# Up projection of a gated MLP by seven products with partial sums in PSUM, in a phase of its own, on one Trainium2 core

## The chip, the cores and the metric

The kernel runs on one core of one Trainium2 chip. The metric is device time in microseconds, as a median of runs. The core has five instruction streams that work side by side: TensorE (PE in the profile; PEld is its weight load), VectorE (DVE), ScalarE (ACT), GpSimd (POOL) and SyncE (SP), which here only starts transfers. TensorE writes into PSUM, eight banks of 128 x 512 fp32 numbers; VectorE and ScalarE read these; GpSimd works here on SBUF alone.

## What is computed

The inputs are x (2048 rows of 512), all in fp32. With xn = layernorm(x):

```python
qkv = xn @ wqkv                      # 512 -> 3*512, 32 heads of 16
# each position attends to 8 positions: itself and 2, 4, ..., 14 rows before it
logits = einsum(q, gathered k) * 16**-0.5 ;  attn = softmax(logits)
s = (attn applied to gathered v) @ wo            # 512 -> 512
h = relu(xn @ w1 + b1) ** 2                      # 512 -> 1792 : "up"
g = silu(h @ w2 + b2)                            # 1792 -> 512 : "down"
out = x + s * g
```

Every product is made with each operand as a sum of a high part (fp32r, a rounded copy) and a low part (operand minus high part): three matmuls, high*high, high*low and low*high (`PASSES`), in place of one.

## The kernel before

**Order of the work.** PE, V, A and G (lines 86 and 70 to 84) are wrappers that issue instructions for TensorE, VectorE, ScalarE and GpSimd and keep each engine's own order as written. A planner keeps two clocks, one for TensorE (227 ns for a matmul) and one for VectorE (elements / 0.96 + 170 ns). The attention is a generator (line 232) of VectorE work: for units of 256 rows a multiplication (`pr`, 128 x 2048), a reduction, softmax, a second multiplication (`pv`) and reduction. `pump(margin)` (line 359) takes pieces from it as long as VectorE's clock stays behind TensorE's plus the margin, so that attention fills VectorE between the things that TensorE waits for. `defer` (line 224) holds back ScalarE's part (an exponential, a start of a load) until TensorE's clock has come to a given time. Transfers on SyncE's queue are placed by the framework.

**Phase 1** (lines 539 to 647). x is normalized, turned (first four tiles on TensorE; later ones through a shuffle by DMA, `xb`, and a transpose on VectorE) and split into high (`A.activation`, line 469) and low (`lowx`, line 471). Sixteen tiles of 128 rows by three thirds of wqkv, 12 matmuls each, give q, k, v (`qkv`, line 477), which go out through ScalarE (`stg`) to DRAM and come back in the attention's layout (`load_u`, line 210). The turned tiles 4 to 15 are stored in DRAM as well (`sx`, line 602) and come back later as `xU` (`load_xT`, line 502). w1 and w2 are loaded in blocks of 128 rows of F and split by ScalarE and GpSimd (`next_w`, line 381).

**Phase 2** (lines 721 to 817) goes over four chunks of 512 rows. Per chunk, 14 steps f: `up(c, f)` (line 509) makes one block of h, 12 matmuls into a bank `ph`, after which ScalarE does relu with bias and two squares, and VectorE the low part (`lowh`, line 525); two steps later `down` (line 653) adds it into four banks `pb`, 12 matmuls. Between them lie the output products of the attention (`out_product`, line 689, 12 matmuls per tile, from `oq`, which is read back from `so` in DRAM, turned by VectorE and split) and the end: `gate` (silu) and `finish`, where VectorE multiplies, GpSimd adds x and a store follows. PSUM: four banks `acc`, two `h`, two `tp`.

Of the kernel before, what the change touches and what calls it, by code (L numbers as in the profile page):

```python
# [8 lines left out]
F32 = mybir.dt.float32  # L9
# [12 lines left out]
W = 8  # L22
# [14 lines left out]
Q0, Q1, K0, K1, V0, V1 = range(6)  # L37
HOME = {0: 10, 1: 6, 2: 7, 3: 8, 4: 9, 5: Q0, 6: Q1, 7: K0, 8: K1, 9: V0, 10: V1}
# [4 lines left out]
TURN = 4  # L43

# [8 lines left out]
def body(ctx: ExitStack, tc: tile.TileContext, x, wqkv, wo, w1, b1, w2, b2, out):  # L53
# [42 lines left out]
    xTa = ctx.enter_context(tc.tile_pool(name="xTa", bufs=1))  # L96
    keep = ctx.enter_context(tc.tile_pool(name="keep", bufs=1))
    wts = ctx.enter_context(tc.tile_pool(name="wts", bufs=1))
    hpool = ctx.enter_context(tc.tile_pool(name="ph", bufs=1))
# [5 lines left out]
    def psH(name):  # L105
        return psum.tile([P, 512], F32, name=name, tag="h", bufs=2)
# [23 lines left out]
    p1ctx = ExitStack()  # L130
    px, pstg, pxT = (p1ctx.enter_context(tc.tile_pool(name=n, bufs=1)) for n in ("px", "pstg", "pxT"))
    xins = {}


# [7 lines left out]

    def buffer(name, i):
        return wts.tile([P, 2, 2, 512], FR, name=name, tag=f"b{i}")


    wq = [buffer(f"wq{i}", i) for i in range(6)]
# [15 lines left out]
    def wq_parts(s, kt):  # L163
        w = wq[2 * s + kt // 2]
        return w[:, 0, kt % 2], w[:, 1, kt % 2], raws[s, kt]
# [36 lines left out]
    sx = {c: dram.tile([P, TPC, 2, KT, P], F32, name=f"sx{c}") for c in range(1, NCH)}  # L202
# [170 lines left out]
    w12 = {}  # L373

    def load_w(f):
        r1, r2 = (piece(f"{n}{f}") for n in ("w1r", "w2r"))
        dma(r1.rearrange("p (k c) -> p k c", c=P), w1[:, f * P:(f + 1) * P].rearrange("(k p) c -> p k c", p=P))
        dma(r2, w2[f * P:(f + 1) * P, :])
        raws[f] = r1, r2

    def next_w():

        f = len(w12)
        if f < NF:
            w12[f] = buffer(f"w{f}", HOME[f]) if f in HOME else p2.tile([P, 2, 2, 512], FR, name=f"w{f}")
            for i, r in enumerate(raws.pop(f)):
                split(w12[f][:, 0, i], w12[f][:, 1, i], r, G)
            if f + 2 < NF:
                load_w(f + 2)


    NT = S // P
    mv, means, rs, shifts, xn, xb, pTs, xt, xT, seen = ({} for _ in range(10))
# [50 lines left out]
    def place(t):  # L444
        if t < TPC:
            xt[t] = xT[0][:, t]
        else:
            xt[t] = pxT.tile([P, 2, KT, P], FR, name=f"xt{t}", tag="xt", bufs=4)
# [8 lines left out]
    def trans(t):  # L457
        place(t)
        pTs[t] = psT(f"pxT{t}")
# [9 lines left out]
        A.activation(xt[t][:, 0], pTs[t].rearrange("p (k n) -> p k n", k=KT), AF.Copy)  # L469

    def lowx(t):
        not_before(seen.pop(t))
        V.tensor_sub(xt[t][:, 1], pTs.pop(t).rearrange("p (k n) -> p k n", k=KT), xt[t][:, 0].bitcast(F32))
# [3 lines left out]
    def qkv(t, s, between=None, late=False):  # L477
# [5 lines left out]
        for n, (kt, a, b) in enumerate(order):  # L483
            PE.matmul(ps, xt[t][:, a, kt], wq[2 * s + kt // 2][:, b, kt % 2, :], start=n == 0, stop=n == 11)
            if between and n == 5:
                between()
        evacuate(t, s, ps)

    def evacuate(t, s, ps):
        if t % 2 == 0:  # L490
            stgs[s] = pstg.tile([P, 4, 2, P], F32, name=f"stg{t}_{s}", tag="stg", bufs=4)
# [10 lines left out]
    def load_xT(c):  # L502
        xT[c] = xTa.tile([P, TPC, 2, KT, P], FR, name=f"xU{c}", tag="xT")
        for j in range(0, TPC, 2):
            A.dma_start(xT[c][:, j:j + 2].bitcast(F32), sx[c][:, j:j + 2])

    hs = {}

    def up(c, f):
        ph = psH(f"ph{c}_{f}")  # L510
        n = 0
# [5 lines left out]
        if f == NF - 1 and c + 1 < NCH:  # L517
            load_xT(c + 1)
# [320 lines left out]
```

## Time and profile before

| what | value |
| --- | --- |
| median of three runs | 501.14 us (500.05 to 503.08) |
| profiled execution, span | 500.6 us |
| TensorE busy | 491.6 us, 98% |
| VectorE busy | 422.9 us, 84% |
| ScalarE busy | 212.2 us, 42% |
| GpSimd busy | 133.4 us, 27% |
| moved by DMA | 88.79 MB |

All but a few instructions are issued through the wrapper of line 82, so the profile's groups are told apart by the names of their tiles: `pq` is a bank of the qkv product, `ph` of up, `pb` of down, `pw` of the output product; `pr` and `pv` are the attention's products, `L` its weights; `w` are the split blocks of w1 and w2; `z` the gate and the result. A row of a group has engine, operation, output and inputs, shape, count, then busy time and the mean in ns of one, then the idle time in front of them and what ended it. In a timeline the first number is the start and the second the duration, in us. In the rows of stretches come the stretch, its length, the engine's busy time with its number of instructions, the granted clock, the share of DMA and GB/s.

### The profile page before, as it was taken

What the parts mean: (1) busy time and instruction counts of PE and PEld (TensorE: products, weight loads), DVE (VectorE), ACT (ScalarE), POOL (GpSimd) and SP (SyncE); (2) the same over time, 40 slices, a digit from 0 to 9 for tenths busy, and PEclk for the clock granted to TensorE, in tenths of its full rate; (3) what the DMA queues carried; (4) which work ended last, traced back from release to release, by engine and by line L of the source; (5) the groups of instructions that cost most, each with busy time, mean ns of one, the idle gap of its engine ahead of it and who ended that gap; (6) DMA issues with size and microseconds to landing.
All of it is one profiled execution on the core that took longest, in us unless ns stands there. A gap on an engine that the chain in (4) does not pass through costs nothing.

```text
span 500.6 us, 5874 instructions
## 1 busy us (share of the span) xinstructions
PE 491.6 (98%) x2154; PEld 402.8 (80%) x2154; DVE 422.9 (84%) x352; ACT 212.2 (42%) x377; POOL 133.4 (27%) x123
## 2 busy tenths in 40 slices
PE   8997999999999999999999999999999999999997
PEld 6876888888888888888888888888888888888886
DVE  5905599999889699997999998899999889996235
ACT  5526556652344465515424342441254256214331
POOL 1312255343427499200223002041300022220000
PEclk9998999999999999999999999999999999999999
DMA  8996989969966975644216416152333705121022
GB/s 292 283 287 187 324 293 332 289 200 331 310 234 236 206 252 140 201 168 158 101 26 241 156 44 259 67 216 68 117 126 97 269 2 199 43 84 64 22 84 85
DMA packets 48520, 88.79 MB, mean 177 GB/s; under 512 B 5372, under 2 KB 32364, under 8 KB 45676
## 3 DMA queue, kind: packets, MB, share of 16 engines
q1 hardware_dynamic: 44172, 54.87, 35.1%
q10 hardware_dynamic: 4320, 33.56, 18.8%
q8 instruction: 17, 0.28, 0.2%
q14 instruction: 11, 0.09, 0.0%
HBM read 57.94 MB, written 27.32 MB: 170 GB/s over the span
## 4 chain that ended last, share of the span: by engine, by line
PE 95%; DMA 3%; ACT 0%; DVE 0%; SPq 0%; issue 0%; POOL 0%; ACTq 0%; POOLq 0%
PE ph L82 30%; PE pb L82 30%; PE pq L82 25%; PE pw L82 9%; DMA xb<-xn 2%; DMA x<-in_A_x 1%; PE pxT L82 0%; SPq L455 0%; ACT scratch L82 0%; DVE z L82 0%; ACT xn L82 0%; DVE st L82 0%; POOL rs L82 0%; ACT stg L82 0%; DVE xn L82 0%
## 5 line engine op out<-in xcount | busy, mean ns | idle before, releaser
L82 PE MATMUL pb<-w,h 128*128 128x512 f32 x672 | 160.6, 389 | 0.0
L82 PEld LDWEIGHTS pb<-w,h 128*128 128x128 f32 x672 | 126.1, 188 | 26.2
L82 PE MATMUL ph<-xU,w 128*128 128x512 f32 x504 | 120.6, 389 | 0.0
L82 PEld LDWEIGHTS ph<-xU,w 128*128 128x128 f32 x504 | 94.6, 188 | 19.6
L82 ACT ACTIVATE ph<-ph,b1t 128x512 f32<-128x512 f32 x56 | 37.0, 660 | 159.6 <-PE ph L82 150.6
L82 PE MATMUL pq<-wq,xt 128*128 128x512 f32 x432 | 101.3, 395 | 0.0
L82 PEld LDWEIGHTS pq<-wq,xt 128*128 128x128 f32 x432 | 81.1, 188 | 19.7
L82 DVE TENSOR_TENSOR pr<-k,q 128x2048 f32<-128x2048 f32 x32 | 77.6, 2425 | 1.6 <-DMA q<-sq 1.2
L82 DVE TENSOR_TENSOR pv<-v,L 128x2048 f32<-128x2048 f32 x32 | 74.2, 2320 | 0.6
L82 DVE TENSOR_REDUCE L<-pr 128x128 f32<-128x2048 f32 x32 | 72.9, 2278 | 0.6
L82 DVE TENSOR_REDUCE v<-pv 128x256 f32<-128x2048 f32 x32 | 72.9, 2279 | 0.6
L82 DVE TENSOR_TENSOR h<-ph,h 128x512 fp32r<-128x512 f32 x56 | 38.0, 679 | 31.9 <-ACT ph L82 31.9
L82 PE MATMUL pw<-wot,oT 128*128 128x512 f32 (+1 forms) x204 | 45.9, 376 | 0.0
L82 POOL TENSOR_TENSOR z<-z,xr 128x512 f32<-128x512 f32 x12 | 25.5, 2127 | 67.1 <-DVE z L82 57.7
L82 PEld LDWEIGHTS pw<-wot,oT 128*128 128x128 f32 x204 | 36.8, 188 | 7.1
L82 ACT ACTIVATE stg<-pq 128x512 f32<-128x512 f32 x48 | 28.2, 593 | 31.4 <-PE pq L82 28.0
L82 POOL TENSOR_TENSOR w<-w1r,w 128x512 fp32r<-128x512 f32 x14 | 29.4, 2098 | 44.9 <-ACT w L82 40.0
L82 PE MATMUL ph<-xT,w 128*128 128x512 f32 x168 | 40.5, 390 | 0.0
L82 PEld LDWEIGHTS ph<-xT,w 128*128 128x128 f32 x168 | 31.5, 188 | 6.7
L82 PE MATMUL pq<-wq,xT 128*128 128x512 f32 x132 | 32.7, 408 | 3.6 <-ACT stg L82 3.6
L82 ACT ACTIVATE h<-ph 128x512 fp32r<-128x512 f32 x56 | 33.7, 602 | 1.8
L82 PEld LDWEIGHTS pq<-wq,xT 128*128 128x128 f32 x132 | 25.5, 196 | 10.3 <-ACT stg L82 4.1
(64 smaller groups left out, 330.4 us busy)
## 6 DMA issues: line engine op xcount, KB each, us to landing
k<-sk ACTq DMA_DIRECT2D x8, 1408.0 KB, 8.3
v<-sv ACTq DMA_DIRECT2D x8, 1408.0 KB, 6.5
sx<-xt SPq DMA_DIRECT2D x12, 512.0 KB, 6.2
xU<-sx ACTq DMA_DIRECT2D x6, 1024.0 KB, 8.6
x<-in_A_x SPq DMA_DIRECT2D x16, 256.0 KB, 4.5
sk<-stg SPq DMA_DIRECT2D x8, 512.0 KB, 4.5
sq<-stg SPq DMA_DIRECT2D x8, 512.0 KB, 5.8
q<-sq ACTq DMA_DIRECT2D x8, 512.0 KB, 9.0
```

Source lines behind the costliest of these rows:

```text
L82: return tc.keep_in_program_order(f(*a, **k))
```

## The change

**Up by seven products.** Up is taken out of the chunks and becomes a phase between qkv and down. w1 is taken in pairs of blocks (7 pairs of 2 x 128 columns, rows in two halves of 256) and x in pairs of tiles (rows in two halves of 128, columns in two halves of 256). Four blocks of the product of a 2 x 2 by a 2 x 2 block matrix come from seven block products in place of eight, with sums of blocks made beforehand: `sums` for x (one subtraction on VectorE, three operations on GpSimd) and `sums_parts` (high on ScalarE, low on GpSimd); `prep_a` and `prep_b` for w1. A group is (half of x's pairs, pair of blocks of w1): four pairs of tiles side by side, 512 columns, seven products of two halves of 128 rows by three passes, 42 matmuls. There are 14 groups.

**Partial sums stay in PSUM.** Three banks serve a group. Products are added to a bank which ScalarE or VectorE has already read: ScalarE copies a partial sum out with the bias (`c1`, `c2`), VectorE adds another bank to the copy, TensorE adds the next product to the bank. Two of the seven products of a group are issued within the group behind it.

**Relu passes through DRAM.** A block of up is stored after relu in `sr` (56 stores of 256 KB) and read back in the down phase (`load_h`); there `prep_h` squares twice on ScalarE and subtracts on GpSimd (it was VectorE).

**Space.** x's parts lie in `XA` (four pairs) and `XB` (the other four, through DRAM in `sx`, over the place of wqkv's parts); w1's parts in a ring of three, of which two are later h's buffers; w2's parts take `XA`'s place at the end of up. PSUM has six banks `acc` and two `tp`. Split blocks of w2 are made from the last groups of up to step 7 of the first chunk, by GpSimd and, for five of them, VectorE. Down has 14 steps per chunk with no up between them.

```diff
-Q0, Q1, K0, K1, V0, V1 = range(6)
+SLOT = {p: p if p < 2 else 2 + p % 2 for p in range(NP)}
+HERE, AWAY = (0, 1, 6, 7), (2, 3, 4, 5)
+A11, A12, A22, S1, S2, S3, S4 = range(7)
+B11, B21, B22, T1, T4, T3, T2 = range(7)
+GROUPS = [(0, 0), (0, 1), (0, 2), (1, 0), (1, 1), (1, 2), (0, 3), (0, 4), (1, 3), (0, 5), (1, 4), (0, 6), (1, 5), (1, 6)]
+PREP = {0: 2, 5: 3, 6: 4, 7: 5, 10: 6}
+RELU = 3000
...
-        return psum.tile([P, 512], F32, name=name, tag="acc", bufs=4)
+        return psum.tile([P, 512], F32, name=name, tag="acc", bufs=6)
...
+    def prep_a(fp):
+        W = ring(fp)
+        l, r = halves(fp)
+        A.activation(W[:, B11:B22, 0], l, AF.Copy)
+        A.activation(W[:, B22, 0], r[:, 1], AF.Copy)
+        G.tensor_sub(W[:, B11:B22, 1], l, W[:, B11:B22, 0].bitcast(F32))
+        G.tensor_sub(W[:, B22, 1], r[:, 1], W[:, B22, 0].bitcast(F32))
+        G.tensor_sub(l[:, 0], r[:, 0], l[:, 0])
+        G.tensor_sub(r[:, 0], r[:, 1], r[:, 0])
+        G.tensor_sub(r[:, 1], r[:, 1], l[:, 0])
+        G.tensor_sub(l[:, 1], l[:, 1], r[:, 1])
+
+    def prep_b(fp):
+        W = ring(fp)
+        for n, src in zip((T1, T3), halves(fp)):
+            A.activation(W[:, n:n + 2, 0], src, AF.Copy)
+            G.tensor_sub(W[:, n:n + 2, 1], src, W[:, n:n + 2, 0].bitcast(F32))
...
+    def sums(p):
+        a, b = (pTs.pop(t) for t in (2 * p, 2 * p + 1))
+        if p < TURN // 2:
...
+            A.activation(b, turn, AF.Copy)
+        t = xs[p]
+        V.tensor_sub(t[:, 2:], turned(a, slice(0, D), "p (b k n) -> p b k n"), t[:, :2])
+        G.tensor_add(t[:, 0], t[:, 0], t[:, 1])
+        G.tensor_add(t[:, 3], t[:, 2], t[:, 3])
+        G.tensor_sub(t[:, 1], t[:, 1], t[:, 2])
+
+    def sums_parts(p):
+        x, t = XA[:, SLOT[p]], xs.pop(p)
+        A.activation(x[:, S1:, 0], t, AF.Copy)
+        G.tensor_sub(x[:, S1:, 1], t, x[:, S1:, 0].bitcast(F32))
+        if p in AWAY:
+            dma(sx[p], x.rearrange("p c h k n -> p (c h k n)").bitcast(F32))
...
-    def lowh(f):
-        h, ph, t = hs[f]
-        not_before(t)
-        V.tensor_sub(h[:, 1], ph, h[:, 0].bitcast(F32))
...
+    def product(ps, W, w, X, x, start, stop):
+        n = 0
+        for k in range(2):
+            for a, b in PASSES:
+                PE.matmul(ps.rearrange("p (j n) -> p j n", n=P), W[:, w, a, k], X[:, :, x, b, k], start=start and n == 0,
+                          stop=stop and n == 5, skip_group_check=True)
+                n += 1
...
+    def relu(f, i, ab, z):
+        def go():
+            A.activation(z, z, AF.Relu)
+            out_r(f, i, ab, z)
+        defer(clock["V"] + RELU, go)
...
+    for gi in range(len(GROUPS) + 1):
...
+            product(ps, R, B11, X, A11, True, False)
+            A.activation(c1[:, 0], ps, AF.Identity, bias=bias(f1))
+            pump(LATE)
+        if before:
+            i0, fp0, R0, X0, ps0, c10, c20, q0 = before
+            not_before(held[0])
+            V.tensor_add(c20[:, 1], c20[:, 1], q0)
+            relu(2 * fp0 + 1, i0, 1, c20[:, 1])
+            product(ps0, R0, T4, X0, A22, False, True)
+            A.activation(c10[:, 1], ps0, AF.Relu, bias=bias(2 * fp0))
+            out_r(2 * fp0, i0, 1, c10[:, 1])
+            pump(LATE)
+        if gi in PREP:
+            prep_a(PREP[gi])
+        if group:
+            product(py, R, B21, X, A12, True, True)
+            pump(LATE)
+            V.tensor_add(c1[:, 0], c1[:, 0], py)
+            relu(f1, i, 0, c1[:, 0])
+            product(ps, R, T2, X, S2, False, False)
+            A.activation(c2[:, 0], ps, AF.Identity, bias=bias(f2))
+            pump(LATE)
+            product(q, R, T1, X, S1, True, False)
+            pump(LATE)
+        if before:
+            product(q0, R0, B22, X0, S4, False, True)
+            pump(LATE)
+            V.tensor_add(c20[:, 0], c20[:, 0], q0)
+            relu(2 * fp0 + 1, i0, 0, c20[:, 0])
+        if gi in PREP:
+            prep_b(PREP[gi])
...
+        if gi >= 13:
+            next_w2(G)
+            next_w2(V if gi == 13 else G)
+        if group:
+            product(ps, R, T3, X, S3, False, False)
+            A.activation(c2[:, 1], ps, AF.Identity, bias=bias(f2))
+            held[:] = [clock["PE"] + 900]
+            pump(LATE)
+            before = (i, fp, R, X, ps, c1, c2, q)
+        if gi == 13:
+            next_w2(G)
+            next_w2(G)
...
+    def prep_h(n, eng=None):
+        if n < NS:
+            hs[n] = h = hbuf[n % 4]
+            r = rbuf.pop(n)
+            A.activation(h[:, 0], r, AF.Square)
+            A.activation(r, r, AF.Square)
+            (eng or G).tensor_sub(h[:, 1], r, h[:, 0].bitcast(F32))
...
+        def step(f):
+            n = c * NF + f
+            prep_h(n + 2)
+            load_h(n + 3)
             if c == 0:
-                next_w()
-            up(c, f)
+                next_w2(V if f % 2 else G)
...
+                if 3 <= f < 7:
+                    split(wot[:, 0, f - 3], wot[:, 1, f - 3], rwo[(f - 3) // 2][:, (f - 3) % 2], G)
```

In phase 1 `sums(p)` is called behind the second `lowx` of a pair and `sums_parts(p)` behind the next product; `prep_a` and `prep_b` of the first two pairs of blocks lie in its last four rounds. The output products of three tiles of the chunk before move to steps 1, 6 and 8, and the last chunk keeps its three last steps for the end, tile by tile, as before.

More of the change, by code (lines that the diff above doesn't have):

```diff
@@ L458, in trans @@
         place(t)
-        pTs[t] = psT(f"pxT{t}")
+        if t < TURN or t % 2 == 0:
+            pTs[t] = psT(f"pxT{t}")
+        else:
+            xs[t // 2] = stgp.tile([P, 4, 2, P], F32, name=f"xs{t}", tag="stg", bufs=5)
+            pTs[t] = xs[t // 2][:, :2].rearrange("p b k n -> p (b k n)")
         if t < TURN:
@@ L575, in body @@
     constants()
+    sums(0)
     qkv(0, 0, lambda: highs(2, 0))
@@ L584, in body @@
     lowx(3)
+    sums(1)
+    sums_parts(0)
     stats(4)
@@ L588, in body @@
     qkv(0, 2)
+    sums_parts(1)
     norm(4)
@@ L613, in body @@
             trans(a + 2)
+        else:
+            load_away(0)
         pump(LATE)
@@ new lines, in view @@
+    def view(base, off, shape, **k):
+        n = 1
+        for d in k.values():
+            n *= d
+        return base[:, off:off + n].rearrange(shape, **k)
+    W0f, W1f = (rings[i].rearrange("p c h k n -> p (c h k n)") for i in (0, 1))
+    hbuf = [view(b, o, "p (h n) -> p h n", h=2, n=512) for b, o in ((W1f, 0), (W1f, 1024), (W1f, 2048), (W0f, 0))]
+    pxc2.close()
+    x21c.close()
+    p2 = ctx.enter_context(tc.tile_pool(name="p2", bufs=1, side="right"))
+    wot = p2.tile([P, 2, 4, 512], FR, name="wot")
@@ L715, in finish @@
         dma(tile_rows(out, t)[:, cols], z[:, cols])
-    wot = p2.tile([P, 2, 4, 512], FR, name="wot")
-    b2t = p2.tile([P, D], F32, name="b2t")
     dma(b2t, b2[None, :].to_broadcast([P, D]))
+    rwo = [p2.tile([P, 2, D], F32, name=f"rwo{i}", tag="rwo", bufs=2) for i in range(2)]
+    for i in range(2):
+        for q in range(4):
+            rows = wo[q * P + 64 * i:q * P + 64 * i + 64, :].rearrange("(g p) n -> p g n", g=2)
+            dma(rwo[i][32 * q:32 * q + 32], rows)
+    for n in range(3):
+        load_h(n)
+    prep_h(0)
+    prep_h(1)
     for c in range(NCH):
@@ L725, in body @@
         room = ROOM if c else ROOM0
-        for f in range(2, NF):
+        def step(f):
+            n = c * NF + f
+            prep_h(n + 2)
+            load_h(n + 3)
             if c == 0:
-                next_w()
-            up(c, f)
-            pump()
-            if c == 0 and f == 3:
-                rwo = [p2.tile([P, 2, D], F32, name=f"rwo{i}", tag="oT", bufs=2) for i in range(2)]
-                for i in range(2):
-                    for q in range(4):
-                        rows = wo[q * P + 64 * i:q * P + 64 * i + 64, :].rearrange("(g p) n -> p g n", g=2)
-                        dma(rwo[i][32 * q:32 * q + 32], rows)
+                next_w2(V if f % 2 else G)
+        for half in ((0, 1), (2, 3)):
+            for f in range(2):
+                if half[0] == 0:
+                    step(f)
+                for j in half:
+                    down(pb, c, f, j)
+                pump(room)
+            if half[0] == 0 and c:
+                out_product(t0 - 3, psT(f"pw{t0 - 3}"))
+                pump(room)
+        if c:
+            load_o(c * 2 - 1, True)
+        for f in range(2, NF - 3 if last else NF):
+            step(f)
             if c == 0:
-                if 6 <= f < 10:
-                    split(wot[:, 0, f - 6], wot[:, 1, f - 6], rwo[(f - 6) // 2][:, (f - 6) % 2], G)
+                if 3 <= f < 7:
+                    split(wot[:, 0, f - 3], wot[:, 1, f - 3], rwo[(f - 3) // 2][:, (f - 3) % 2], G)
             elif f == 2:
```

302 lines of the change are left out of this document (176 added, 126 removed).

## The prediction

> **What bounds the kernel now.** I read the page's busy shares and its chain of waits first, then that chain in order of time, then the groups by form, then stretches and timelines of VectorE (DVE) and GpSimd (POOL), the two engines that the change loads differently.
>
> ```profile
> span 500.6 us, 5874 instructions
> PE 491.6 (98%) x2154; PEld 402.8 (80%) x2154; DVE 422.9 (84%) x352; ACT 212.2 (42%) x377; POOL 133.4 (27%) x123
> PE 95%; DMA 3%; ACT 0%; DVE 0%; SPq 0%; issue 0%; POOL 0%; ACTq 0%; POOLq 0%
> ```
> ```profile
> 154.01 2.76 PE ph L82 x12
> 156.77 2.72 PE pb L82 x12
> ```
>
> TensorE is the path for 95% of the span, and twelve 512-column matmuls take 2.72 us: 227 ns each, back to back. So a matmul taken out is worth 227 ns, as long as nothing else becomes late. Two more views say what may become late.
>
> ```profile
> 45.40:457.60 412.20, 384.51 (x281) 1.00 0.54 179
> ```
>
> That is DVE from its first attention product to its last: 384.5 us of work in 412.2, so 27.7 us idle. DVE is nearly a second bound. What it may lose is read at the end:
>
> ```profile
> 457.62 0.53 SPq L312 DMA_DIRECT2D so<-v  x1
> 457.82 0.69 DVE L82 TENSOR_TENSOR h<-ph,h 128x512 fp32r<-128x512 f32 x1 [0.23 <-ACT ph L82]
> ...
> 460.65 2.52 SPq L674 DMA_DIRECT2D oq<-so  x4
> ...
> 463.15 1.08 ACT L82 ACTIVATE oT<-pT 128x512 fp32r<-128x512 f32 x2
> 463.87 1.28 DVE L82 TENSOR_TENSOR oT<-pT,oT 128x512 fp32r<-128x512 f32 x2
> ...
> 479.58 0.69 DVE L82 TENSOR_TENSOR h<-ph,h 128x512 fp32r<-128x512 f32 x1 [4.75 <-ACT ph L82]
> ...
> 491.16 5.75 PE L82 MATMUL pw<-wot,oT 128*128 128x512 f32 x36
> ```
> ```profile
> oq<-so SPq DMA_DIRECT2D x32, 128.0 KB, 3.4
> ```
>
> The last attention unit is stored at 457.6. Its four reads begin at 460.7, take 2.5 us to issue and 3.4 to land (466.0, taking one issue as 0.6), a transpose, a copy and a subtraction of some 0.65 us each follow (468.0), and from the start of the last output products to the end there are 500.6 - 491.2 = 9.4 us. DVE by itself would let the kernel end at 477.5: **23 us of room before, and after a gain of 19 only 4.**
>
> **The products.**
>
> ```profile
> L82 PE MATMUL ph<-xU,w 128*128 128x512 f32 x504 | 120.6, 389 | 0.0
> L82 PE MATMUL ph<-xT,w 128*128 128x512 f32 x168 | 40.5, 390 | 0.0
> L82 DVE TENSOR_TENSOR h<-ph,h 128x512 fp32r<-128x512 f32 x56 | 38.0, 679 | 31.9 <-ACT ph L82 31.9
> L82 DVE TENSOR_TENSOR z<-pb,b2t 128x512 f32<-128x512 f32 x16 | 10.5, 683 | 2.7 <-PE pb L82 2.6
> L82 ACT ACTIVATE ph<-ph,b1t 128x512 f32<-128x512 f32 x56 | 37.0, 660 | 159.6 <-PE ph L82 150.6 <-DVE pv L82 4.5 <-DVE mx_None L82 4.5
> L82 DVE TENSOR_TENSOR z<-z,xlast 128x256 f32<-128x256 f32 x2 | 0.9, 426 | 0.1
> L82 ACT ACTIVATE h<-ph 128x512 fp32r<-128x512 f32 x56 | 33.7, 602 | 1.8
> L82 POOL TENSOR_TENSOR w<-w1r,w 128x512 fp32r<-128x512 f32 x14 | 29.4, 2098 | 44.9 <-ACT w L82 40.0 <-DMA x<-in_A_x 4.9
> L82 POOL TENSOR_TENSOR w<-w2r,w 128x512 fp32r<-128x512 f32 x14 | 22.6, 1615 | 0.0
> ```
>
> Up has 504 + 168 = 672 matmuls. After the change it has 14 groups of seven products of six: 588. The operands keep their form (128x128 weights, four runs of 128 columns), so 84 matmuls at 227 ns go: **-19.0 us**, and TensorE alone would end at 481.6. All else is priced against that.
>
> **Inside the up phase** a group lasts 42 x 0.227 = 9.5 us. ScalarE has four copies out of PSUM (0.66 each, the row with b1t) and three relus (0.60, as h<-ph) in it, 4.4 us, and in five groups four copies of parts more: it fits. DVE has three additions (0.68, the row of z<-pb). But sums are added to a bank that has just been copied out: the sixth product of a group waits for a DVE addition, and the product on the group before waits for ScalarE's last copy, one product (1.36 us) after it was produced, so 0.66 us of copy and a hand-off have 1.36 us. A small operation in front (0.6) is hidden there, just. Parts of w1 come from POOL, 5.5 operations of 512 columns for each pair of blocks; in three places (pairs three, four and six) the first use is one group, 9.5 us, behind the start. At 1.3 us each that is 7.1 us, at 1.9 (below) 10.5: about 1 us late each time. I take **+3** (bounds: 0, all hidden; 14 x 2.3, one attention operation in front of an addition in every group, 32).
>
> **POOL and DVE.** POOL loses the 28 splits (52.0 us) and gets, in operations of 512 columns: sums and parts of x 28 (3.5 for each of eight pairs), parts of w1 38.5, splits of w2 nine, and the 56 subtractions for h, which were DVE's: 131.5. What that costs is in this stretch, where POOL had no pause, and in a free DVE row:
>
> ```profile
> 178.77 3.34 POOL L82 TENSOR_TENSOR w<-w1r,w 128x512 fp32r<-128x512 f32 x1
> 182.07 1.30 POOL L82 TENSOR_TENSOR w<-w2r,w 128x512 fp32r<-128x512 f32 x1
> 183.34 1.29 POOL L82 TENSOR_TENSOR wot<-rwo,wot 128x512 fp32r<-128x512 f32 x1
> 184.59 3.34 POOL L82 TENSOR_TENSOR w<-w1r,w 128x512 fp32r<-128x512 f32 x1
> ```
> ```profile
> 183.19 0.68 DVE L82 TENSOR_TENSOR h<-ph,h 128x512 fp32r<-128x512 f32 x1
> 183.79 2.98 DVE L82 TENSOR_TENSOR pr<-k,q 128x2048 f32<-128x2048 f32 x1
> 186.81 2.29 DVE L82 TENSOR_REDUCE L<-pr 128x128 f32<-128x2048 f32 x1
> 189.61 2.97 DVE L82 TENSOR_TENSOR pr<-k,q 128x2048 f32<-128x2048 f32 x1
> ...
> 242.20 2.29 DVE L82 TENSOR_TENSOR pr<-k,q 128x2048 f32<-128x2048 f32 x1
> ```
>
> An attention multiplication takes 2.98 instead of 2.29 us when a POOL operation is running at its start, and the POOL operation behind it waits until it has ended (3.34 instead of 1.29). The reduction keeps its 2.29. With a full queue POOL does three operations in 184.59 - 178.77 = 5.82 us: 1.94 us each.
>
> The Trainium skill ("SBUF — State Buffer", "Who interferes with whom") says why: a DVE instruction with two SBUF inputs and a GpSimd instruction that reads SBUF exclude one another for a whole instruction, whichever starts first. By that rule the additions from PSUM cost nothing extra; the rows agree (0.68 us for h<-ph while POOL is busy), and the rule speaks against handing DVE's work to POOL. Taken strictly it gives the time of rival 2 below; by the rows of before it gives two fifths of that loss.
>
> **The down phase on POOL.** A step of 12 matmuls is 2.72 us. In steps 0 to 7 of the first chunk POOL has eight subtractions for h, four splits of w2 and four of wo: 16 x 1.94 = 31.0 us in 21.8. Two steps of lead (5.4) cover part: **+4** (bounds: 0, at 1.29 each it is 20.6; and 9). At the change of phase the first h can be ready only behind what POOL still has of w2 (three or so at 1.3 to 1.9, against some 2 us of lead): **+2** (0 to 5). Later chunks have 14 + 4 + 2 operations in 49 us, 39 at 1.94: hidden, with no other cover than that. h's way through DRAM (14.7 MB out and back) puts reads on SyncE's queue behind stores that wait for DVE and POOL; those have about four steps (10.9 us) of lead against 3.4 to land and 3 for copies and POOL, so they are hidden until DVE is 4 us late; past that they pass its lateness on.
>
> **The start.**
>
> ```profile
> 23.81 0.78 POOL L82 TENSOR_TENSOR rs<-rs,mhalf 128x1 f32<-128x1 f32 x1 [0.45 <-DVE rs L82]
> ...
> 25.63 2.75 SPq L455 DMA_DIRECT2D xb<-xn  x4
> ...
> 38.28 0.73 DVE L82 STREAM_TRANSPOSE pxT<-xb 128x512 f32<-128x512 f32 x1 [13.10 <-DMA xb<-xn]
> ...
> 45.43 2.28 DVE L82 TENSOR_TENSOR pr<-k,q 128x2048 f32<-128x2048 f32 x1
> ```
> ```profile
> PE pq L82 <- ACT stg L82: 3.6, 1, 3.6
> ```
>
> Sums of the first two pairs (3 + 2 operations of 512 columns on POOL, 1.29 each, 6.5 us) now stand in front of the last rs at 23.8, and so of the shuffle, the transpose at 38.3 and DVE's first attention product at 45.4. POOL pauses there too, so +0 to +6.5; I take 2.5 for DVE. TensorE's only stall in the middle, 3.6 us for a bank, now has six banks in place of four: from -3.6 to +3, taken **0**. x goes to DRAM in 1.8 MB per pair, for four pairs, in place of 1.0 for six:
>
> ```profile
> 50.00:75.00 25.00, 25.00 (x109) 1.00 0.93 309
> ```
>
> At 309 GB/s and 93% busy a shuffle behind one lands up to 6 us later. I take 0, since w2's 0.5 MB per pair leave the same stretch.
>
> **Two sums.** TensorE's way: 500.6 - 19.0 + 3 + 4 + 2 = 490.6. DVE's way, from 477.5: work -38.0 + 42 x 0.68 + 8 x 0.68 (sums) + 5 x 0.68 (splits of w2) + 8 x 0.17 (subtractions of x cut into two of 0.43) = +0.8; five of the removed subtractions, the two shown and three between, lay behind 457.6, so before it +4.2; start +2.5; of the 27.7 us idle recovered -5 (bounds 0 and -27.7; the waits for ScalarE, 31.9 over the span, go, and waits for products come). The exclusion: POOL with 131.5 + some 40 unchanged operations at 1.29 (221 us) in the 412 - 64 x 2.28 = 266 us that the multiplications leave: 0.83 of 64 starts meet one, at 0.69 us 37 us. The same arithmetic for before (68 operations) gives 14.6, where the rows below show 32 x 0.145 + 32 x 0.04 = 5.9.
>
> ```profile
> L82 DVE TENSOR_TENSOR pr<-k,q 128x2048 f32<-128x2048 f32 x32 | 77.6, 2425 | 1.6 <-DMA q<-sq 1.2
> L82 DVE TENSOR_TENSOR pv<-v,L 128x2048 f32<-128x2048 f32 x32 | 74.2, 2320 | 0.6
> ```
>
> So I take 40%, 15, and +9 net (0 to +31). 477.5 + 4.2 + 2.5 - 5 + 9 = 488.2. The two ways hold each other up less than they add, since a waiting TensorE lets DVE catch up: 490.6. The median of the runs is 501.14 beside this span of 500.6, so +0.5: **491 us**.
>
> **Rivals.** (1) All is hidden: 481.6 + 0.5 = 482. For it: ScalarE and POOL have idle time for all of it. Against it: the 4 us of DVE's room and 31 us of POOL work in 21.8. (2) The exclusion decides, one mechanism with its place in the attention multiplications: net +31 and no idle time recovered, 477.5 + 4.2 + 2.5 + 31 = 515; it overtakes TensorE's way from a DVE growth of 13, and the whole gain is gone at 23. For it: POOL's queue is full half of the time. Against it: before, only two fifths of such a count came true. I put it at 498 to 515, on either side of before. (3) The hand-offs in PSUM: with one multiplication (2.3) in front of DVE's addition in every group 14 x 2.3 = 32 and 514; gain gone at 1.36 us per group. For it: the sixth product has little lead, and ScalarE's relus wait on DVE in order. Against it: DVE's 679 ns subtractions stood in a like place before, and the longest wait of TensorE was the 3.6 us above. That fewer matmuls are run than before is fixed by the program; only their 227 ns could change, and no operand's form does.
>
> **How the numbers follow.** The forecast (486 to 498) 0.50, rival 1 0.17, rival 2 0.21, rival 3 0.12. A difference under 0.5% (498.6 to 503.6) can't be told from none. Faster: 0.48 + 0.17 + 0.02 = 0.67; same: 0.02 + 0.09 + 0.02 = 0.13; slower: 0.10 + 0.10 = 0.20. The range goes from 481, rival 1 with a little of the bank stall won back, to 507, which leaves out about half of rivals 2 and 3; the forecast's own is 486 to 498.
>
> **What would show it.** 588 matmuls into the banks of up at 227 ns; in a list of TensorE's waits, ScalarE's copies of c1 or c2 and DVE's additions with 3 us in all, POOL's h with 6, most of it in the first chunk; multiplications with a mean near 2.5 us; the last store of attention near 467, less than 25 us before the end. Wrong would be the forecast if TensorE waits in every group, if these means go to 2.9, or if the stall near 36 to 40 us grows to more than 5.

## The result, and the profile after

The changed kernel takes 559.2 us (median of 4 runs, 558.3 to 560.7) where the kernel before takes 502.1 beside it (4 runs, 500.1 to 503.4): the ratio is 1.114, with a 95% interval of 1.110 to 1.118. It is slower by some 57 us. The forecast was 491, its range 481 to 507, and its likeliest sign was wrong.

The page of the changed kernel, with span, busy times, granted clock in 40 slices, and the chain that ended last:

```profile
span 558.9 us, 6206 instructions
PE 496.0 (89%) x2070; PEld 399.0 (71%) x2070; DVE 443.3 (79%) x359; ACT 253.8 (45%) x449; POOL 301.5 (54%) x248
PEclk9997998897997699987998997989999999999999
PE 41%; POOL 16%; issue 14%; DMA 5%; DVE 4%; ACT 4%; SPq 1%; ACTq 0%; POOLq 0%; DVEq 0%
```

TensorE was 95% of that chain and is now 41%. Its time falls into two parts. It stands still for 558.9 - 496.0 = 62.9 us; before, that was 500.6 - 491.6 = 9.0. And it is busy for 496.0 us, although the products that were taken out should have left 491.6 - 19.0 = 472.6. So of the 77.3 us above the 481.6 that TensorE alone would need, **53.9 are new standstill and 23.4 are slower matmuls**. The digits of PEclk below 9 are the slices in which the clock was lower.

TensorE's list of waits (what it waited for: us in total, times, longest) says where it stood:

```profile
PE X L91 <- ACT c L91: 24.9, 7, 9.8
PE pq L91 <- ACT XA L91: 15.1, 5, 6.1
PE pb L91 <- POOL ring L91: 11.0, 7, 3.2
PE pb L91 <- ACT ring L91: 6.4, 1, 6.4
```

X are products of the up phase, pq those of the projections in front of it, pb those of the down phase: 57.4 us in 20 waits. ScalarE (ACT) is named for 46.4 of them, an engine that is busy 45% of the time. What ScalarE and GpSimd waited for in turn:

```profile
ACT ring L91 <- POOL w1r L91: 32.1, 6, 12.7
ACT XA L91 <- POOL xs L91: 24.5, 7, 5.3
ACT scratch L91 <- POOL mean L91: 21.5, 5, 7.5
```

The longest of these in order of time, in the up phase (start, duration, instruction, and in brackets the idle time before it with what ended it):

```profile
180.04 1.07 POOL L91 TENSOR_TENSOR L<-L,mx_None 128x512 f32<-128x512 f32 x1 [5.46 <-DVE mx_None L91]
181.07 4.00 POOL L91 TENSOR_TENSOR ring<-w1r,ring 128x512 fp32r<-128x512 f32 x2
...
186.63 1.52 POOL L91 TENSOR_TENSOR w1r<-w1r,w1r 128x256 f32<-128x256 f32 x2
188.19 0.63 ACT L91 ACTIVATE ring<-w1r 128x512 fp32r<-128x512 f32 x1 [12.69 <-POOL w1r L91]
...
189.24 1.25 ACT L91 ACTIVATE c<-X,b1t 128x512 f32<-128x512 f32 x2
...
189.97 2.92 PE L91 MATMUL X<-XA,ring 128*128 128x512 f32 x6 [9.80 <-ACT c L91]
```

Read from the bottom: six matmuls wait 9.8 us for a copy c out of PSUM; two such copies take 1.25 us. The copy is late because ScalarE, which works in order, had a copy of w1's parts (ring<-w1r, from prep_b) in front of it and waited 12.7 us there for GpSimd's sums. GpSimd in turn had stood for 5.5 us in front of an operation of the attention that waited for VectorE, then did two subtractions in 4.0 us (beside VectorE's multiplications) and the four sums. And the six matmuls take 2.92 us; six at full clock take 1.52. In the stage before it the same happens with the first parts of w1 and the sums of x:

```profile
113.42 2.00 POOL L91 TENSOR_TENSOR ring<-w1r,ring 128x512 fp32r<-128x512 f32 x2
115.37 2.79 POOL L91 TENSOR_TENSOR w1r<-w1r,w1r 128x256 f32<-128x256 f32 x1
...
120.57 2.40 POOL L91 TENSOR_TENSOR XA<-xs,XA 128x1024 fp32r<-128x1024 f32 x1
122.94 0.23 POOL L91 TENSOR_SCALAR mean<-mean 128x1 f32<-128x1 f32 x1
```
```profile
117.49 0.71 DVE L91 STREAM_TRANSPOSE pxT<-xb 128x512 f32<-128x512 f32 x1
...
123.20 0.72 ACT L91 ACTIVATE scratch<-x,mean 128x512 f32<-128x512 f32 x1 [7.55 <-POOL mean L91]
...
129.18 0.59 ACT L91 ACTIVATE XA<-pxT 128x512 fp32r<-128x512 f32 x1
...
129.82 4.51 PE L91 MATMUL pq<-XB,XA 128*128 128x512 f32 x12 [6.10 <-ACT XA L91]
```

A 0.23 us mean of one column, which the norm needs, stands behind nine and a half microseconds of GpSimd's new work, and ScalarE's norm waits 7.6 us for it. The tile that TensorE waits 6.1 us for is not made from this mean: it was turned by 118.2, but its copy (XA<-pxT) stands behind that norm in ScalarE's order and starts at 129.2.

By stages (TensorE's first product of up at 164.6, of down at 342.4; columns: length, then busy time of TensorE, its weight loads, VectorE, ScalarE and GpSimd, then the granted clock):

```profile
0.00:164.60 164.60, 147.68 (x606) 117.20 (x607) 116.22 (x123) 75.13 (x151) 85.84 (x109) 0.94 0.76 249
164.60:342.40 177.80, 146.47 (x590) 117.14 (x588) 143.93 (x100) 76.62 (x133) 73.14 (x57) 0.91 0.63 218
342.40:558.90 216.50, 201.81 (x876) 164.70 (x876) 183.17 (x137) 102.08 (x166) 142.51 (x84) 0.98 0.59 187
```

The 588 products of up need 588 x 0.227 = 133.5 us and the stage lasts 177.8, so this one stage is 44 us too long. VectorE's groups, for the rows of before:

```profile
L91 DVE TENSOR_TENSOR pr<-k,q 128x2048 f32<-128x2048 f32 x32 | 86.5, 2703 | 0.3
L91 DVE TENSOR_TENSOR pv<-v,L 128x2048 f32<-128x2048 f32 x32 | 79.1, 2473 | 1.4 <-POOL L L91 1.2
```

The multiplications grew by 32 x (0.278 + 0.153) = 13.8 us, but VectorE is busy for only 443.3 of 558.9 us.

### The profile page after: what moved, and what is told of

It is laid out like the page before. It is cut to its first block, busy times and chain, and to the rows that moved or that the text cites. A ratio compares the mean times of both kernels' runs of the same rounds, so it can differ in the third digit from the quotient of the medians.

```text
span 558.9 us, 6206 instructions
## 1 busy us (share of the span) xinstructions
PE 496.0 (89%) x2070; PEld 399.0 (71%) x2070; DVE 443.3 (79%) x359; ACT 253.8 (45%) x449; POOL 301.5 (54%) x248
## 4 chain that ended last, share of the span: by engine, by line
PE 41%; POOL 16%; issue 14%; DMA 5%; DVE 4%; ACT 4%; SPq 1%; ACTq 0%; POOLq 0%; DVEq 0%
PE pb L91 22%; PE pw L91 8%; PE X L91 6%; POOL ring L91 6%; POOL w1r L91 5%; PE Z L91 2%; PE Y L91 2%; DMA r<-sr 2%; POOL XA L91 2%; DMA w2r<-in_B_w 1%; DVE pr L91 1%; ACT XA L91 1%; DMA sx<-XA 1%; DVE xs L91 1%; POOL xs L91 1%
## 5 line engine op out<-in xcount | busy, mean ns | idle before, releaser
L91 PE MATMUL pb<-XA,ring 128*128 128x512 f32 x672 | 160.3, 397 | 17.4 <-POOL ring L91 11.0
L91 PEld LDWEIGHTS pb<-XA,ring 128*128 128x128 f32 x672 | 127.9, 191 | 47.6 <-POOL ring L91 14.2
L91 PE MATMUL pq<-XB,XA 128*128 128x512 f32 x420 | 108.7, 412 | 15.1 <-ACT XA L91 15.1
L91 POOL TENSOR_TENSOR ring<-r,ring 128x512 fp32r<-128x512 f32 x56 | 93.2, 1685 | 37.0 <-ACT r L91 28.2
L91 PEld LDWEIGHTS pq<-XB,XA 128*128 128x128 f32 x420 | 82.8, 199 | 36.3 <-ACT XA L91 17.2
L91 POOL TENSOR_TENSOR ring<-w1r,ring 128x512 fp32r<-128x512 f32 (+1 forms) x28 | 43.2, 1564 | 46.6 <-ACT ring L91 43.8
L91 ACT ACTIVATE c<-X,b1t 128x512 f32<-128x512 f32 x56 | 38.1, 686 | 61.5 <-PE X L91 42.3
L91 PE MATMUL X<-XA,ring 128*128 128x512 f32 x168 | 47.0, 423 | 18.4 <-ACT c L91 18.4
L91 PE MATMUL X<-XB,ring 128*128 128x512 f32 x168 | 43.4, 401 | 6.5 <-ACT c L91 6.5
L91 PE MATMUL pq<-XB,xt 128*128 128x512 f32 x144 | 37.6, 394 | 0.2 <-DVE xt L91 0.2
```

The lines of the kernel that those rows point to most:

```text
L91: return tc.keep_in_program_order(f(*a, **k))
```

## The experiments

The first theory, Q: GpSimd's queue, worked through in order, and ScalarE in order behind it, are what TensorE waits for. Its rivals: the hand-offs of sums in PSUM (H, rival 3 of the prediction), GpSimd and VectorE excluding one another (rival 2), and later T, the transfers, h's way through DRAM above all. A time without an interval below is of one run; the kernel before took 499.9 to 503.9 us in the runs beside them.

**GpSimd's four sums of w1 left out.**

```diff
-        G.tensor_sub(l[:, 0], r[:, 0], l[:, 0])
-        G.tensor_sub(r[:, 0], r[:, 1], r[:, 0])
-        G.tensor_sub(r[:, 1], r[:, 1], l[:, 0])
-        G.tensor_sub(l[:, 1], l[:, 1], r[:, 1])
```

> The changed kernel without the four sums of w1's blocks that GpSimd makes for every pair (the parts T1 to T4 are then parts of the raw blocks: the values of up are not the reference's; every other instruction stays). Theory Q (in the up phase ScalarE's copies of the sums wait in order for GpSimd, and TensorE waits for ScalarE's copies out of PSUM behind them): the up phase, 177.8 us from its first product to the first of down, falls to 135 to 150, TensorE's waits for copies of c fall from 24.9 us to under 8, the span to 515 to 532. Theory H (the hand-offs in PSUM themselves are too short, one product of 1.36 us for copy and signal): the waits for c stay over 18 us and the up phase over 165. Theory D (transfers of the parts and of relu stop the phase): nothing changes, up 170 to 178.

Measured: 537.4 us. The up stage went from 177.8 to 156.7 us, TensorE's waits for the copies c from 24.9 to 5.9. That is 23 us of operations (GpSimd's busy time went from 301.5 to 278.1) on an engine that is half idle, and they were worth 22 us of the end. The waits fell as theory Q expected; the stage and the span (535.6) stayed a little above its bounds of 150 and 532.

**The same operations, with lead.** Nothing is left out; the second half of the preparation comes one group after the first, and the groups are ordered so that a pair of blocks is used later, two groups or more behind the start of its preparation.

```diff
-GROUPS = [(0, 0), (0, 1), (0, 2), (1, 0), (1, 1), (1, 2), (0, 3), (0, 4), (1, 3), (0, 5), (1, 4), (0, 6), (1, 5), (1, 6)]
-PREP = {0: 2, 5: 3, 6: 4, 7: 5, 10: 6}
+GROUPS = [(0, 0), (0, 1), (1, 0), (0, 2), (1, 1), (1, 2), (0, 3), (1, 3), (0, 4), (1, 4), (0, 5), (1, 5), (0, 6), (1, 6)]
+PREP = {0: 2, 4: 3, 6: 4, 8: 5, 10: 6}
...
-        if gi in PREP:
-            prep_b(PREP[gi])
+        if gi - 1 in PREP:
+            prep_b(PREP[gi - 1])
```

> The changed kernel with another order alone: the groups are taken so that each pair of w1's blocks is used in two groups closer to one another, its sums are begun two groups ahead of the first use, and the second half of the preparation (ScalarE's copies of the sums) is issued one group behind the first. Same instructions, same result. Theory Q: ScalarE no longer meets unfinished sums: up 135 to 148 us in place of 177.8, span 515 to 530. Theory H: up over 165. Theory G (GpSimd lacks throughput in this phase, not lead): up 160 to 178, with waits moved from the copies to the products.

Measured: 540.4 us, the up stage 157.6, above theory Q's bound of 148 and below what H (over 165) and G (160 to 178) expected; TensorE's waits for c fell from 24.9 to 5.6. In that kernel the middle of the stage is nearly without a gap:

```profile
195.00:310.00 115.00, 114.71 (x497) 94.20 (x496) 107.91 (x80) 58.84 (x100) 51.13 (x38) 0.98 0.61 204
```

114.7 us of products in 115.0, with every hand-off in PSUM still there: **H falls.** VectorE's busy time is 443.1, the same as before the reordering, while the stage is 20 us shorter, so those 20 us weren't lost to the exclusion between GpSimd and VectorE either. Who stands in front of whom in an in-order queue is enough for them.

**GpSimd's work on the sums of x left out** (ScalarE copies in place of the subtraction):

```diff
-        G.tensor_add(t[:, 0], t[:, 0], t[:, 1])
-        G.tensor_add(t[:, 3], t[:, 2], t[:, 3])
-        G.tensor_sub(t[:, 1], t[:, 1], t[:, 2])
...
-        G.tensor_sub(x[:, S1:, 1], t, x[:, S1:, 0].bitcast(F32))
+        A.activation(x[:, S1:, 1], t, AF.Copy)
```

> The changed kernel without GpSimd's work on the sums of x's parts: the three sums are left out, and the low half of the four summed parts is a copy by ScalarE (1.06 us) in place of a subtraction by GpSimd; values of up are then not the reference's. Transfers stay as they are. Theory Q: the first phase, 164.6 us before its last product, falls to 149 to 154; the later phases change little (span 543 to 550). Theory D (the 1.8 MB stores stand in front of the shuffles): it stays at 160 to 165.

Measured: 540.3 us. The stage before up went from 164.6 to 147.2, the waits of pq from 15.1 to 2.9; both the stage and the span (538.5) came out somewhat shorter than theory Q expected.

**GpSimd's subtraction for h's low part left out.**

```diff
-            (eng or G).tensor_sub(h[:, 1], r, h[:, 0].bitcast(F32))
```

> The changed kernel without GpSimd's subtraction for h's low part in the down phase (the low part keeps what lay there, so the result is not the reference's; matmuls and transfers stay). Theory Q (GpSimd's queue): the down phase, 216.5 us, falls to 200 to 206, TensorE's waits for GpSimd's ring tiles (11.0 us) go, multiplications of the attention get shorter there (the whole mean of pr from 2.70 to under 2.60). Theory D (h comes back from DRAM too late): the waits stay but for ScalarE's squares, and the phase stays over 211.

Measured: 554.0 us. The down stage went from 216.5 to 206.9 and the waits for GpSimd's h went, but the waits for ScalarE's h, 6.4 us, grew to 9.8. The stage lies just above theory Q's bounds (200 to 206) and below D's (over 211): here GpSimd isn't all.

**The stage before up in another order.** The sums of x stand behind the norm's operations, a product later, and prep_a and prep_b two rounds later; nothing is left out.

```diff
-        if more:
-            sums_parts(a // 2 + 1)
...
+        if a > 2:
+            sums_g(a // 2)
+        if a > 2:
+            sums_parts(a // 2)
...
-        elif a == 8:
+        if a == 10:
             prep_a(0)
-        elif a == 10:
+        elif a == 12:
             prep_b(0)
```

> The changed kernel with the same instructions, in phase 1 issued in another order alone: GpSimd's three sums and the summed parts of a pair come a round later, behind the operations that the norm of the next tiles waits for and behind their shuffle; those of the first two pairs come after the first shuffle; the preparation of w1's first pair moves one round later too. Theory Q (order in GpSimd's queue, and ScalarE waiting behind it, not its total work): phase 1 falls from 164.6 to 148 to 153 us and TensorE's waits for ScalarE's copies of x's parts from 15.1 to under 5; up and down stay within 4 us; span 541 to 549. Theory G (GpSimd's and VectorE's throughput with the exclusion): 157 to 165.

Measured: 541.2 us; the stage took 151.6, as theory Q expected. That is 13 of the 17 us that leaving the work out gave.

**The start of down in another order**: the first two blocks of h are read and prepared inside the last two groups of up, the last splits of w2 move into the steps of down, three of them go to VectorE in place of GpSimd, and wo is split at steps 9 to 12.

```diff
+        if gi == len(GROUPS):
+            prep_h(0)
+            prep_h(1)
...
-        if gi >= 13:
+        if gi == 13:
+            for n in range(3):
+                load_h(n)
+        if gi == 13:
...
-                next_w2(V if f % 2 else G)
+                next_w2(V if f % 4 else G)
...
-                if 3 <= f < 7:
+                if 9 <= f < 13:
```

> The changed kernel with the same work, from the last group of up on in another order alone: only the four blocks of w2 that are there are split in the last group, so that ScalarE no longer waits for the transfer of more; the first two blocks of h are read back one group earlier and prepared first; the remaining splits of w2 go one to a step, seven to VectorE and three to GpSimd, those of wo to steps 9 to 12. Theory Q: the wait of 6.4 us for h at the start of down goes, TensorE's waits for GpSimd there fall from 11.0 to under 5 us, down from 216.5 to 202 to 209, span 543 to 552. Theory D (the way of h through DRAM): down stays over 212.

Measured: 555.5 us. Up and down together went from 394.3 to 388.9 us, and the down stage by itself was no shorter (220.5); TensorE still waited 9.3 us for GpSimd and 4.1 for ScalarE there. A miss: 3.7 us of the whole is no more than the kernel before varies by, and this order of the work did not mend down.

**All three orders together.**

> The three changes of order together (groups and preparation, phase 1, down), nothing left out, result as the reference's. If the losses lie in three places that do not hide one another (theory Q): phase 1 148 to 153, up 140 to 152, down 202 to 209, span 492 to 513, so near the kernel before. If they hide one another (VectorE or GpSimd throughput is the bound behind the waits, theory G): span over 520.

Measured: 527.7 us (526.7 to 528.8; ratio 1.052, 1.047 to 1.057), above what theory Q expected (492 to 513). The stages last 151.9, 148.9 and 226.2 us: the first two lie inside its bounds, down does not, and the span of 527.0 is what theory G had named (over 520). Up is 29 us shorter than in the changed kernel; down is longer. SyncE's queue (SPq), ScalarE and TensorE at its start, in order of time in this kernel:

```profile
306.26 5.18 SPq L922 DMA_DIRECT2D rwo<-in_A_wo  x8
...
312.25 0.82 SPq L742 DMA_DIRECT2D w2r<-in_B_w  x2
313.21 1.18 SPq L725 DMA_DIRECT2D sr<-c  x2
314.45 0.60 SPq L769 DMA_DIRECT2D r<-sr  x1
...
316.39 2.12 SPq L769 DMA_DIRECT2D r<-sr  x4
319.43 0.63 ACT L91 ACTIVATE ring<-r 128x512 fp32r<-128x512 f32 x1 [8.14 <-DMA r<-sr]
...
320.11 1.22 PE L91 MATMUL pb<-XA,ring 128*128 128x512 f32 x2 [4.26 <-ACT ring L91]
```

The read of relu's rows (r<-sr) is issued at 314.5, behind eight loads of wo, two of w2 and two stores of the last groups' relus; ScalarE waits 8.1 us for it and TensorE 4.3. So T may be a cause too, and the next four runs separate it from GpSimd's work, all on the kernel with the three orders.

**GpSimd's sums and subtractions left out as well** (the edits of the first, third and fourth experiment together; its splits of w1, w2 and wo stay):

> The kernel with all three orders (527.0 us of span: 151.9 before the up phase, 148.9 in it, 226.2 from the first product of down to the end), and GpSimd's four sums of w1 blocks, its sums of x and the subtraction for h's low part left out (x's low parts are copies by ScalarE), so the output is another. Theory Q (what is left is GpSimd's work and the engines in order behind it): the down part comes to about 200, up to 140, in all 482 to 495. Rival T (what is left is h's way through DRAM: stores, reads and the loads of w2 and wo on SyncE's one queue): down keeps at least 212, in all 505 to 518, and ScalarE's waits for the reads of r stay near 25 us.

**The way through DRAM left out**: no store of relu's rows, no read; the first square is made from rows of x that stay in SBUF, and a copy stands for the second.

```diff
-        dma(sr[f, i][:, :, ab].rearrange("p c q n -> p c (q n)"), src.rearrange("p (c n) -> p c n", c=2))
...
-            dma(rbuf[n], sr[f, i][:, (AWAY if i else HERE).index(p) // 2].rearrange("p a q n -> p (a q n)"))
...
-            A.activation(r, r, AF.Square)
+            A.activation(r, r, AF.Copy)
```

> The kernel with all three orders, but relu's rows are neither stored to DRAM nor read back: the squares are made from rows of x that lie in SBUF, with the same instructions on ScalarE and GpSimd, so the output is another. Theory T (way through DRAM): the down part goes from 226 to 203 to 213, the first 20 us of it lose their stalls, in all 504 to 514. Theory Q (GpSimd): the waits for GpSimd's h stay (9 us), in all 521 to 528. Both in part: between, 514 to 521.

**Both left out.**

> The kernel with all three orders, with both of the former left out: GpSimd's sums and subtractions for h, and the way of relu's rows through DRAM; the output is another. If these two are all that stands between the kernel and the TensorE's own work, 480 to 488. If the attention's work on VectorE is a bound of its own (rival 2 of the prediction), or ScalarE's order of work, it stays above 495 although GpSimd is nearly idle.

Measured, with the length of the three stages by the profile:

| kernel (each edit but the first two on the three orders) | time, us | before up | up | down to the end | TensorE idle | TensorE busy | clock |
|---|---|---|---|---|---|---|---|
| as changed | 559.2 | 164.6 | 177.8 | 216.5 | 62.9 | 496.0 | 0.945 |
| three orders | 527.7 | 151.9 | 148.9 | 226.2 | 41.0 | 486.0 | 0.968 |
| and no sums and subtractions on GpSimd | 501.9 | 141.7 | 149.6 | 208.7 | 22.1 | 478.0 | 0.982 |
| and no way through DRAM | 510.1 | 151.6 | 148.1 | 208.6 | 24.9 | 483.4 | 0.976 |
| and neither | 487.9 | 140.1 | 146.2 | 199.7 | 14.5 | 471.6 | 0.993 |

The first of the three (501.9) fell between what the two theories expected; the second (510.1) is where T put it, and the third (487.9) at the end of its bounds of 480 to 488. In down each edit alone gives 17.5 us and both 26.5: **GpSimd's work and the way through DRAM hold it up in about equal parts, and partly in the same places.** Whether GpSimd's part in down is its order or its load was not separated; in the changed kernel it had no pause there from 356.9 to 390.9 us (33.90 us of work in 33.96). The rows of the last kernel show that down without them is TensorE's own work:

```profile
0.00:140.13 140.13, 138.27 (x606) 112.44 (x607) 109.20 (x124) 80.71 (x158) 40.59 (x73) 1.00 0.89 295
140.13:286.36 146.23, 137.16 (x590) 112.22 (x588) 137.93 (x98) 77.66 (x133) 52.64 (x31) 0.98 0.43 161
286.36:486.10 199.74, 196.15 (x877) 162.73 (x875) 178.37 (x142) 102.28 (x168) 46.92 (x26) 1.00 0.43 136
```

What stays in up, 146.2 against 133.5, lies mostly in its first part: TensorE waits 5.4 us for x's parts to come back from DRAM and 3.6 for copies c. One limit of the two runs without GpSimd's sums and subtractions: to leave them out also frees VectorE of them (its two multiplications fall to 2.37 and 2.41 us in the first), so the 26 us of the first hold whatever the exclusion costs by way of VectorE; in the reordered kernels above that work was all there.

**wo and b2 loaded later**, from in front of down to its steps 4 to 6; nothing is left out.

```diff
-    dma(b2t, b2[None, :].to_broadcast([P, D]))
-    for i in range(2):
-        for q in range(4):
+    def load_wo(i):
+        for q in range(4):
...
+                if f in (4, 5):
+                    load_wo(f - 4)
+                if f == 6:
+                    dma(b2t, b2[None, :].to_broadcast([P, D]))
```

> The kernel with all three orders, with the loads of wo and b2 moved from in front of the down phase to its steps 4 to 6; every result is as before. Rival T with SyncE's queue as the place: reads of r land earlier at the change of phase, whose stalls (about 12 us between 296 and 350 us) halve: 519 to 523. If the place is not the queue but GpSimd or VectorE's lateness: within 2 us of 527.7.

Measured: 520.0 us (518.8 to 520.9; ratio 1.036, 1.031 to 1.041), as T expected: TensorE's waits for ScalarE's h fell from 7.4 to 0.6 us, those for GpSimd did not (9.4 and 11.1). So the place behind these loads in SyncE's queue is 7.7 of the 17.6 us that the way through DRAM costs. It is the fastest version here that computes everything, and still slower than the kernel before.

**The clock by itself.** In the kernel with neither, ScalarE's copy of the first product of every second group is made twelve times:

```diff
-            A.activation(c1[:, 0], ps, AF.Identity, bias=bias(f1))
+            for _ in range(12 if gi % 2 else 1):
+                A.activation(c1[:, 0], ps, AF.Identity, bias=bias(f1))
```

> The kernel of the run before with neither GpSimd's sums nor the way through DRAM (span 486.1 us, TensorE busy 471.6, granted clock 0.993; its output is another), with ScalarE's copy of the first product of every second group made twelve times in place of once: 11 copies of 0.66 more are 7.3 us, of which 2.7 lie beside two products, so TensorE is to stand still some 4.5 us in seven places, 32 us in all, and does the same matmuls. If the clock drops behind a stall whatever its cause, TensorE's busy time grows by about a third of the added idle time, to 479 to 485, and the six matmuls behind each stall take over 2 us in place of 1.52: in all 523 to 532. If the slower matmuls of the changed kernel come from something else (SBUF reads beside GpSimd, transfers), busy stays at 471 to 474 and the whole at 516 to 522.

Measured: 540.6 us, more than expected, since six of the seven stalls came out at 6.0 us and one at 9.5 instead of 4.5. What the run was for is TensorE's busy time: 483.1 instead of 471.6, for the same matmuls. GpSimd was busy 25% of the time, relu's rows did not pass through DRAM, and both were so in the kernel beside it; so the standstill itself slows the matmuls behind it. One stall with what goes ahead of it and follows it (the copies run from 182.5 to 191.1, and the first row, beside them, is at full speed, so it is not the copies that slow the matmuls):

```profile
183.56 1.52 PE L91 MATMUL Y<-XA,ring 128*128 128x512 f32 x6
191.12 2.93 PE L91 MATMUL X<-XA,ring 128*128 128x512 f32 x6 [6.04 <-ACT c L91]
193.85 2.19 PE L91 MATMUL Z<-XA,ring 128*128 128x512 f32 x6
195.88 1.52 PE L91 MATMUL Z<-XB,ring 128*128 128x512 f32 x6
```

Six matmuls take 2.93 in place of 1.52 us, the next six 2.19, and then they are quick again: some 2 us lost behind 6.0 of standstill.

## Why the prediction was wrong, step by step

- **The products, -19.0: right.** In the kernel with neither, whose output is another but whose matmuls are the same, TensorE is busy 471.6 us, where 491.6 - 19.0 = 472.6 were predicted, and the kernel takes 487.9, near the 482 of rival 1. The gain was there, and four times as much was paid for it elsewhere.
- **Inside up, +3: wrong; the largest error of all** (177.8 us for 133.5 of products, +44). The step "I take +3" made two mistakes. It let ScalarE pass because 4.4 us of work fit into 9.5, and so looked at its load and not at its order: one copy that waits for GpSimd holds the copies c of the group that is running. And it priced GpSimd's parts of w1 as 7.1 to 10.5 us of work without what stands between them in the same queue, operations of the attention that wait for VectorE (5.5 us in the rows above). "About 1 us late each time" was 9.8 at the longest and 24.9 in all. The bound of 32 belonged to another mechanism, the hand-offs in PSUM, and these were hidden in the middle of the second experiment's stage. The lead alone gives back 20 us of the stage, 19 of the whole.
- **The start, TensorE 0: wrong.** The stall of 3.6 us for a bank did go, but up to 45.6 us TensorE waited 3.5 us for ScalarE's copy of x's parts instead, and VectorE's first attention product came 3.6 us later (49.0 instead of 45.4, +2.5 predicted). But past the start the stage had no term at all. The sums of x and the first parts of w1 were counted as operations of GpSimd and not put in front of the norm's small ones behind them, nor the norm in front of ScalarE's copies behind it; the stage lasts 164.6 us, 151.6 with them in another order and 140.1 in the kernel with neither.
- **Down, +4 and +2: too small by more than half.** Against the kernel with neither cause the stage is 16.8 us longer. GpSimd's subtractions cost 9.6 of it by themselves, inside the bounds (0 to 9 and 0 to 5). What failed is the sentence that the reads have "about four steps of lead" and "are hidden until DVE is 4 us late": at the change of phase they have none, because SyncE's queue has the stores of the last relus, w2 and wo in front of them. That is so in the rows of the three orders, and without the way through DRAM that kernel gains 17.6 us. In the changed kernel itself the longest wait, 6.4 us at the change of phase (+2, bounds 0 to 5), stood behind another load of the same queue, and not behind GpSimd: ScalarE waited 4.7 us for a transfer of w2, with h's copy in order behind it:

```profile
340.51 1.31 ACT L91 ACTIVATE XA<-w2r 128x512 fp32r<-128x512 f32 x2 [4.65 <-DMA w2r<-in_B_w]
341.72 0.61 ACT L91 ACTIVATE ring<-r 128x512 fp32r<-128x512 f32 x1
...
342.39 1.22 PE L91 MATMUL pb<-XA,ring 128*128 128x512 f32 x2 [6.39 <-ACT ring L91]
```

- **No term for the clock: 23.4 us missing.** All waits were priced at their own length; that "only their 227 ns could change" was written down and given no term. Here every microsecond of new standstill brought 23.4 / 53.9 = 0.43 us of slower matmuls. The Trainium skill ("TensorE: Matmul & The Clock Gate", Part 1) says that the array falls to half its clock after an idle window of about 3.4 us and needs as long to come back; by it six matmuls would take an estimated 2.7 us (six times twice 227 ns), and the rows are near it (2.92 and 2.93). On the idle window the runs differ from it, as the last section shows. A price for this belonged into the sum, and it was left out.
- **POOL and DVE, +9: a fair size.** It measured 13.8, and the multiplications had a mean of 2.59 ("near 2.5", wrong at 2.9). But VectorE's way of 488 was no bound: its last attention store is at 527.7, 31 us before the end, and from 385.1 us to the end of its last matmul at 555.2 TensorE stands still once, for 1.1 us. Rival 2 as what decides falls by that, and by the second experiment, in which 20 us of the stage went while VectorE's busy time stayed.
- **The sign.** Rivals 2 (498 to 515) and 3 (514) put a chance on slower, each as the one mechanism that decides. What came were the order of the queues in the first two stages, GpSimd's work and the way through DRAM in the last, and the clock on top. No rival was "GpSimd's queue, with ScalarE behind it", although the prediction had counted 131.5 operations of 512 columns into that queue, whose busy time went from 133.4 to 301.5 us. And none of its three signs of being wrong came, though the time was 68 us off: TensorE waited for c in 7 places and not in every one of the 14 groups, the multiplications stayed under 2.9, and no stall near 36 to 40 us grew past 5. They watched the rivals and not this mechanism.

## What to carry to other kernels

Before work is handed to an engine with idle time, write down its queue in order, with what each neighbour waits for, and then the same for every in-order engine that waits for it: a 0.7 us operation behind a 12 us wait costs what it blocks, not what it lasts. When a transfer is added, look at which transfers stand in front of it in its queue at the change of phase, where the lead of the steady state doesn't hold. And a kernel in which TensorE never stops has a clock to lose: price each stall at its length and, from about 1.5 us on, at up to some 2 us more, since it can slow the matmuls behind it, as the next section shows.

## What was not expected of the hardware

**A stall's length and its place decide whether the clock goes.** In each of the 14 traces the granted clock changes only at points that lie whole multiples of 3.41 us apart, wherever the stalls are, and it is full or half of full. Cut at these points, every trace shows the same. Of the stretches at full clock in which TensorE was busy for less than 45% of the time, all 82 were followed by a stretch at half clock; of the 1874 in which it was busy for more than 55%, none was; between these, 3 of 16. From half clock it came back only behind a stretch with TensorE busy for 85% or more.

So a stall of 2.04 us in the changed kernel (239.97 to 242.01) slowed the matmuls behind it, and one of 3.10 us in the kernel of the last experiment (142.79 to 145.89) did not. First the one, then the other, in such stretches (length, TensorE's busy time and matmuls, granted clock, DMA share and GB/s):

```profile
238.87:242.28 3.41, 1.37 (x6) 1.00 0.33 102
242.28:245.70 3.42, 3.42 (x9) 0.50 0.99 378
245.70:249.11 3.41, 3.41 (x16) 1.00 0.94 273
```
```profile
140.62:144.04 3.42, 2.17 (x10) 1.00 0.94 346
144.04:147.45 3.41, 1.56 (x7) 1.00 0.99 374
147.45:150.86 3.41, 3.41 (x17) 1.00 0.99 359
```

The first lies whole in one stretch and leaves it 40% busy; the second is cut in two by a border, which leaves 63% and 46%. By these figures a stall under some 1.5 us (45% of 3.41) does nothing by itself, one over some 3.8 us (twice 55% of 3.41) always costs, and between them its place decides; no run moved a stall alone to try it. The price is half of the time for which TensorE is busy at half clock, 1.7 us for one full stretch. In the changed kernel it was busy for 46.0 us at half clock: half of that is 23.0 us, and before it was 1.7. So the clock makes up 21.3 of the 23.4 us of slower matmuls above.

**One multiplication can take twice its free time.** Of the 32 products pr of the changed kernel (shortest, median and longest in ns, then the first and the last start), the median is that of a free row, and the longest is not:

```profile
L91 DVE TENSOR_TENSOR pr<-k,q x32: 2227/2294/4497, 49.0 to 469.3; 128x2048 f32<-128x2048 f32 x32
```

4.50 us is 2.2 more than a free multiplication. GpSimd now has operations of 1024 columns of 2.4 us, and the longest multiplication began 0.04 us behind the start of one:

```profile
72.49 2.39 POOL L91 TENSOR_TENSOR XA<-xs,XA 128x1024 fp32r<-128x1024 f32 x1 [1.17 <-ACT XA L91]
```
```profile
72.53 4.50 DVE L91 TENSOR_TENSOR pr<-k,q 128x2048 f32<-128x2048 f32 x1
```

GpSimd's operation ends at 74.9, and from there to the multiplication's end at 77.0 is about one free multiplication: it waited out the whole operation. The second longest, 4.29 us at 157.8, began in such an operation too. In the two kernels without GpSimd's sums the longest pr took 3.27 and 2.92 us.
